# Tokens in runs of nine on two partition halves, early dummy matmuls, bf16 transposes of the token weight and a first token mix by source

## The chip, the cores and the metric

The kernel runs on one core of a Trainium2 chip. The metric is the device time of one execution in microseconds (us). TensorE (PE) multiplies, VectorE (DVE), ScalarE (ACT) and GpSimd (POOL) do elementwise work, and SyncE (SP) issues nearly all DMA. Every engine works through its own instructions in a fixed order that a small scheduler inside the kernel file fixes before the run: an instruction that waits holds up everything behind it on its engine.

Each run is timed beside the kernel before on the same chip. A ratio is the mean time of a kernel's fast runs over the mean of the fast runs of before of the same rounds, so it is not quite the ratio of the medians that are quoted. Where one of a kernel's executions was in the slow state, the median quoted here is that of its fast ones; the recorded expectations still quote medians of all (410.1 and 406.3 us for runs 4 and 5).

## The reference

```python
# q, k, v: [8 batches, 8 heads, 576 tokens, 64], f32
kv  = einsum('bhsd,bhse->bhde', k, v)
out = einsum('bhsd,bhde->bhse', q, kv)
x   = out / sqrt(mean(out*out, -1) + 1e-6) * g_norm      # -> [8, 576, 512]
a1  = alpha1 * x + beta1
u   = x + lam * einsum('ts,bsd->btd', w_tok, a1)         # token mix, w_tok 576x576
a2  = alpha2 * u + beta2
y   = u + lam * (relu(a2 @ w_ch1) @ w_ch2)               # channel mix, 512 -> 2048 -> 512
```

## The kernel before

Operations are recorded with their inputs, outputs and an estimated cost, put in order by the scheduler, and only then emitted. 576 tokens do not fill partitions evenly: 512 of them go on 128 partitions in runs of four, and the other 64 are a tail on 64 partitions, with packets of 256 bytes.

```python
def load_main(tile, key, src, b, hs, at=None):          # 128 partitions, 1 KB packets
    P.op("SP", 0.6, lambda e: e.dma_start(
        tile[:, hs].rearrange("p h c d -> p h (c d)"),
        src[b, hs, 0:512, :].rearrange("h (p c) d -> p h (c d)", c=4)), ...)

def load_tail(tile, key, src, b, lo, at=None):          # 64 partitions, 256 B packets
    P.op("SP", 0.7, lambda e: e.dma_start(
        tile[lo:lo + 64, :, :], src[b, :, 512:576, :].rearrange("h s d -> s h d")), ...)
```

From batch 2 on, q is split in two bf16 parts (`qs`: high part on ACT, rest on DVE or POOL) and transposed by DMA (`qt <- qs`). The product of k and v (`kv`) is evicted as two bf16 parts too (`kvd`), by ACT and DVE. Behind q times kv come a norm, a multiplication that makes the input of the token mix (`rt`), and the token mix.

```python
def split_q(b):
    for c in range(5):
        ...
        P.op("ACT", act_us(512), lambda e, ...: copy(e, hi, src), r=kin, w=[kh])
        P.op(dve_pool(512), 0, lambda e, ...: e.tensor_tensor(      # DVE or POOL
            out=lo, in0=src, in1=hi, op=ALU.subtract), r=kin + [kh], w=[kl])
...
P.op(dve_pool(64 * m), 0, lambda e: e.tensor_tensor(                # rt: DVE or POOL
    out=r_, in0=x, in1=eb, op=ALU.mult), ..., pri=-100)
...
P.op("SP", 0.6, lambda e: e.dma_start(out[b, c:512:4, :], x), r=keys, dma_us=0.8)   # one store
```

The scheduler's choice between two engines, its model of a DMA and its dummy matmuls (which fill PE's idle time before the first channel mix, once a zeroed tile `wz` is there):

```python
mine = t + o.cost[e] + (self.spare if e == "DVE" and "POOL" in o.eng else 0.0)
...
if at + o.cost[e2] < mine: return True                   # the other engine is better
...
dma_free = max(dma_free, t) + pick.lat                   # loads
pick.end = dma_free + 2.0
```

Of the kernel before, what the change touches and what calls it, by code (L numbers as in the profile page):

```python
# [22 lines left out]
class Op:  # L23
    __slots__ = ("eng", "cost", "fn", "deps", "alloc", "tiles", "pri", "idx",
                 "start", "end", "pos", "waits", "inc", "lat", "ring", "clock")

    def __init__(self, eng, cost, fn, pri, idx):
        self.eng, self.cost, self.fn, self.pri, self.idx = eng, cost, fn, pri, idx
        self.deps = set()
        self.alloc, self.tiles = [], []  # L30
        self.start = self.end = self.pos = None
        self.waits, self.inc, self.lat, self.clock, self.ring = [], False, None, None, None
# [3 lines left out]


# [10 lines left out]
class Prog:  # L48
# [20 lines left out]
    def op(self, eng, cost, fn, r=(), w=(), pri=0.0, dma_us=None, at=None):  # L69
# [4 lines left out]
        if at is not None:  # L74
            o.pri = at
        self.ops.append(o)
        for key in r:
# [24 lines left out]
    def hasten(self, targets):  # L102
# [11 lines left out]
        for o, way in rank.items():  # L114
            if o not in targets and o.eng != "SP":
                o.pri = -1000.0 - way

    def schedule(self):
# [25 lines left out]
        def place(tile, t):  # L144
# [5 lines left out]
            c = [b for b in range(8) if bank_ok(b, t)]  # L150
            if not c:
                return None
# [9 lines left out]
        def better_elsewhere(o, e, t):  # L162

            mine = t + o.cost[e] + (self.spare if e == "DVE" and "POOL" in o.eng else 0.0)
            for e2 in o.eng:
# [8 lines left out]
                if at + o.cost[e2] < mine:  # L174
                    return True
            return False

        while left:
            progressed = False
            for e, q in queues.items():  # L180
                while q and free[e] <= t + 1e-9:
                    pick = None
                    first = self.warm and self.warm[0].start is None
                    cands = q[:self.pe_window] if e == "PE" and not first else q[:400]
                    for o in cands:
# [6 lines left out]
                    if pick is None and e == "PE" and first:  # L192

                        tile = self.ptile(1)
                        pick = self.op("PE", 0.22, lambda e, tile=tile: self.warm[1](e, tile),
# [23 lines left out]
                    if pick.lat is not None:  # L219
                        if e == "SP":  # L220
                            dma_free = max(dma_free, t) + pick.lat
                            pick.end = dma_free + 2.0
                        else:
                            pick.end = t + pick.lat + 2.3
# [106 lines left out]
def bass_transnormer_attn__then__resmlp_affine_kernel(  # L331
# [15 lines left out]
    with ExitStack() as stack:  # L347
# [5 lines left out]
        with nc.sbuf_tensor("qtr", [128, 20, 128], F32R) as qtr:  # L353
            pass
# [5 lines left out]
        wz = sb("wz", [128, 512], BF16)  # L360
        smask = sb("smask", [128, 128], BF16)
        emask = sb("emask", [33, 128], BF16)
        ab2 = sb("ab2", [128, 8], F32)
        b2hl = sb("b2hl", [128, 4, 2], BF16)
        bias = sb("bias", [128, 16], F32)
        e1_bc = sb("e1_bc", [128, DM], F32)
# [3 lines left out]
        eps = sb("eps", [128, 1], F32)  # L370
        kf = sb("kf", [128, NH, 4, DH], F32)
        vf = sb("vf", [128, NH, 4, DH], F32)
        qf = sb("qf", [128, NH, 4, DH], F32)
        kft = sb("kft", [128, NH, DH], F32)
        qft = sb("qft", [128, NH, DH], F32)
# [19 lines left out]
        erow = stg[0:33, 1, 0:2, :]  # L395
        ebf = stg[0:33, 1, 2, 0:256].bitcast(BF16)
        pcol = stg[0:8, 2, 3, 0:128]
        grow = stg[0:1, 2, 3, 128:192]
        ones = stg[0:1, 2, 3, 192:320]
        wst, wst2 = hst[:, 0:2048], hst[:, 2048:2880]  # L400
# [31 lines left out]
        def load_main(tile, key, src, b, hs, at=None):  # L432
            P.op("SP", 0.6, lambda e: e.dma_start(
                tile[:, hs].rearrange("p h c d -> p h (c d)"),
                src[b, hs, 0:512, :].rearrange("h (p c) d -> p h (c d)", c=4)),
                w=[(key, a) for a in halves(hs)],
                dma_us=2.8 * (hs.stop - hs.start) / 8, at=at)

        def load_tail(tile, key, src, b, lo, at=None):
            P.op("SP", 0.7, lambda e: e.dma_start(  # L440
                tile[lo:lo + 64, :, :], src[b, :, 512:576, :].rearrange("h s d -> s h d")),
                w=[key], dma_us=0.55, at=at)

        def load_kv(b, parts=ALL, at=None):
            for i, hs in enumerate(parts):
                for tile, src, n in ((kf, k, "k"), (vf, v, "v")):
                    load_main(tile, n + "f", src, b, hs, at=at and at(n, i))
                    if i == 0:
                        load_tail(kft, n + "ft", src, b, 0 if n == "k" else 64,
                                  at=at and at(n + "t", i))  # L450

        def load_q(b, parts=ALL, at=None):
            for i, hs in enumerate(parts):
                load_main(qf, "qf", q, b, hs, at=at and at("q", i))
                if i == 0:
                    load_tail(qft, "qft%d" % (b % 2), q, b, 64 * (b % 2),
                              at=at and at("qt", i))

        def round_kv(b, parts=ALL):
            for i, hs in enumerate(parts):  # L460
                m = 256 * (hs.stop - hs.start)
                aa = halves(hs)
                for src, dst, lo, n in ((kf, kr, 0, "k"), (vf, vr, 64, "v")):
                    o, s = dst[:, 0:4, hs, :], src[:, hs].rearrange("p h c d -> p c h d")
                    ot, st = dst[0:64, 4, hs, :], kft[lo:lo + 64, hs]
                    P.op(act_dve(m, 1.7) if b < R32 else "DVE", dve_us(m, 1.7),
                         lambda e, o=o, s=s: copy(e, o, s),
                         r=[(n + "f", a) for a in aa], w=[(n + "r", a, 0) for a in aa])
                    P.op(act_dve(m // 4, 1.7) if b < R32 else "DVE", dve_us(m // 4, 1.7),
                         lambda e, o=ot, s=st: copy(e, o, s),  # L470
                         r=[n + "ft"], w=[(n + "r", a, 1) for a in aa])

        def split_q(b):

            lo_, par = 64 * (b % 2), b % 2
            for c in range(5):
                rows = slice(0, 128) if c < 4 else slice(lo_, lo_ + 64)
                src = qf[:, :, c, :] if c < 4 else qft[rows]
                hi, lo = qs[rows, c, :, 0, :], qs[rows, c, :, 1, :]
                kin = [("qf", 0), ("qf", 1)] if c < 4 else ["qft%d" % par]  # L480
# [15 lines left out]
        def qt_groups(b):  # L496

            def group(a, cp):
                t = P.ptile(1)
                lo = 64 * (b % 2)  # L500

                def f(e):
                    for i in range(4 if cp < 2 else 2):
                        if cp < 2:
                            m = e.transpose(t.flat()[:, 128 * i:128 * i + 128],
                                            qf[:, 4 * a + i, 2 * cp:2 * cp + 2, :].rearrange(
                                                "p c d -> p (c d)"), ident[:])
                        else:
                            h = 4 * a + 2 * i
                            m = e.transpose(t.flat()[:, 64 * i:64 * i + 64],  # L510
                                            flat(qft[lo:lo + 64, h:h + 2, :]),
                                            ident[lo:lo + 64, lo:lo + 64])
                    return m
                P.op("PE", 0.131 * (4 if cp < 2 else 2), f,
                     r=["ident", ("qf", a) if cp < 2 else "qft%d" % (b % 2)], w=[t])
                if cp < 2:
                    o = qtr[:, 8 * cp + 4 * a:8 * cp + 4 * a + 4, :].rearrange("p h s -> p (h s)")
                    s = lambda: t.flat()
                else:
                    o = qtr[:, 16 + 2 * a:18 + 2 * a, lo:lo + 64]  # L520
                    s = lambda: t.flat()[:, 0:128].rearrange("p (h s) -> p h s", h=2)
                P.op(act_dve(512 if cp < 2 else 128), 0, lambda e: copy(e, o, s()),
# [725 lines left out]
```

## Time and profile before

403.41 us median of three runs (403.21 to 404.55). What matters of the profile:

| | before |
|---|---|
| first channel-mix matmul (L850) | 58.21 us |
| first q times kv product of batch 2 (L614, the first 64-wide one on `kvd`) | 110.17 us |
| from there to the end of the span (400.7 us) | 290.5 us |
| landing of q's transposes, median | 3.8 us |

The page of before: busy time of PE, then the span in 40 slices of 10 us: PE's busy tenths, the granted PE clock in tenths, and what DMA moved; last the chain of waits that ended last, by engine.

```profile
PE 371.5 (93%) x2430; PEld 217.2 (54%) x2222; DVE 243.9 (61%) x355; ACT 154.4 (39%) x267; POOL 140.1 (35%) x105
PE   0999999899499999989999999989999999999995
PEclk9999999999889999999999999999999999999999
GB/s 205 318 315 332 281 353 350 17 131 138 200 290 200 150 101 114 207 149 190 147 210 123 107 101 196 199 39 106 81 78 26 106 52 2 26 119 27 2 52 79
...
PE 75%; DVE 11%; DMA 7%; issue 3%; ACT 1%; SPq 1%
```

PE is busy 93% of the time, and the DMA is near its full rate in the first 70 us (it reaches 353 GB/s). The chain is three quarters PE. Whether PE's time is well spent is told only by the length of its instructions. The timeline of PE before (start in us, length in us, line, operation, operands, count, and in brackets the idle time before it with what ended it):

```profile
9.64 2.50 PE L536 MATMUL ps<-vr,kr 128*128 128x256 f32 x10 [3.42 <-ACT vr L422]
...
44.85 2.64 PE L536 MATMUL ps<-vr,kr 128*128 128x256 f32 x20
...
58.21 1.04 PE L850 MATMUL ps<-a2t,w 128*128 128x256 bf16 x8
```

Ten kv products of 128x256 take 2.50 us at 9.64 us, and twenty take 2.64 us at 44.85 us: the first stage runs at half clock. The clock row shows 9 there all the same: the record of the clock begins at 42 us in this trace.

The timeline of DVE before, where it waits ahead of batch 2's products:

```profile
97.24 0.69 DVE L891 TENSOR_TENSOR xm<-ps,xm 128x512 f32<-128x512 f32 x1 [0.40 <-PE ps L882]
104.25 1.83 DVE L484 TENSOR_TENSOR qs<-qf,qs 128x512 bf16<-128x512 f32 x2 [6.32 <-ACT qs L422]
106.00 0.60 DVE L568 TENSOR_TENSOR kvd<-ps,kvd 64x128 bf16<-64x128 f32 x2
```

DVE is free at 97.9 us, and batch 2's two kv products are done on PE at 98.4 and 100.5 us. But a piece of batch 3's q split stands in front of their eviction (`kvd`) and waits 6.32 us.

### The profile page before, as it was taken

The page shows a single profiled execution, that of the slowest core. Times are in us where ns is not written, and L with a number is a line of the kernel's source. Part 1 is how long each engine was busy: PE and PEld are TensorE (multiplying, and loading weights), DVE is VectorE, ACT ScalarE, POOL GpSimd, SP SyncE. Part 2 cuts the span into 40 slices and gives each one's busy share as a digit, 9 for nine tenths or more (in the row PEclk, how much of TensorE's full clock was granted, in tenths as well). Part 3 has the DMA queues.
Part 4 walks back from the last instruction along what each step waited for, and adds up shares of the span by engine and source line. Part 5 has one row for each costly group of instructions (what it writes and reads, how often), then busy time and mean ns, then how long its engine had stood idle before and what let it go on. Part 6 is the DMA issues. An engine that isn't in the chain of part 4 may idle for free.

```text
span 400.7 us, 5755 instructions
## 1 busy us (share of the span) xinstructions
PE 371.5 (93%) x2430; PEld 217.2 (54%) x2222; DVE 243.9 (61%) x355; ACT 154.4 (39%) x267; POOL 140.1 (35%) x105
## 2 busy tenths in 40 slices
PE   0999999899499999989999999989999999999995
PEld 0775576446277346534765455435774465446642
DVE  6545879995579715994677628982783448350021
ACT  1345646800557004830465006801670048105600
POOL 3434538791317600492036400870062203420000
PEclk9999999999889999999999999999999999999999
DMA  8999999058799533967495337913340410050012
GB/s 205 318 315 332 281 353 350 17 131 138 200 290 200 150 101 114 207 149 190 147 210 123 107 101 196 199 39 106 81 78 26 106 52 2 26 119 27 2 52 79
DMA packets 94713, 59.25 MB, mean 148 GB/s; under 512 B 60817, under 2 KB 85401, under 8 KB 94688
## 3 DMA queue, kind: packets, MB, share of 16 engines
q1 hardware_dynamic: 94656, 58.88, 57.0%
q8 instruction: 18, 0.29, 0.3%
q14 instruction: 7, 0.06, 0.0%
q10 hardware_dynamic: 32, 0.02, 0.0%
HBM read 38.05 MB, written 9.44 MB: 119 GB/s over the span
## 4 chain that ended last, share of the span: by engine, by line
PE 75%; DVE 11%; DMA 7%; issue 3%; ACT 1%; SPq 1%
PE ps L882 27%; PE ps L835 13%; PE ps L820 10%; PE ps L713 7%; PE ps L536 5%; DMA qt<-qs 3%; DVE w L1154 2%; PE ps L614 2%; DVE qs L484 2%; PE ps L324 2%; DMA qf<-in_q_dram 2%; PE ps L1049 2%; DMA kft<-in_v_dram 2%; PE ps L926 2%; DVE rt L683 1%
## 5 line engine op out<-in xcount | busy, mean ns | idle before, releaser
L882 PE MATMUL ps<-w,ht 128*128 128x512 bf16 x559 | 126.8, 379 | 1.0
L809 ACT ACTIVATE ht<-ps,bias 128x640 bf16<-128x640 f32 (+2 forms) x114 | 82.1, 729 | 46.9 <-PE ps L835 35.3
L882 PEld LDWEIGHTS ps<-w,ht 128*128 128x128 bf16 x576 | 55.2, 98 | 63.8
L835 PE MATMUL ps<-a2t,w 128*128 128x320 bf16 x512 | 73.9, 304 | 6.3 <-DVE kvd L568 4.2
L891 DVE TENSOR_TENSOR xm<-ps,xm 128x512 f32<-128x512 f32 x32 | 22.1, 691 | 71.8 <-PE ps L882 71.6
L835 PEld LDWEIGHTS ps<-a2t,w 128*128 128x128 bf16 x512 | 49.8, 99 | 27.6 <-DVE kvd L568 4.6
L685 POOL TENSOR_TENSOR xm<-xm,g_bc 128x1024 f32<-128x1024 f32 (+1 forms) x18 | 40.2, 2236 | 51.6 <-DVE rt L683 50.8
L484 POOL TENSOR_TENSOR qs<-qf,qs 128x512 bf16<-128x512 f32 x15 | 22.5, 1501 | 93.3 <-ACT qs L422 92.9
L820 PE MATMUL ps<-a2t,w 128*128 128x512 bf16 x231 | 53.0, 379 | 0.5
L563 ACT ACTIVATE kvd<-ps 64x128 bf16<-64x128 f32 x24 | 6.5, 271 | 105.3 <-PE ps L536 105.1
L713 PE MATMUL ps<-rt,wt 128*128 128x512 bf16 x172 | 39.3, 379 | 4.7 <-DVE xm L695 2.5
L820 PEld LDWEIGHTS ps<-a2t,w 128*128 128x128 bf16 x240 | 22.8, 98 | 25.8
L713 PEld LDWEIGHTS ps<-rt,wt 128*128 128x128 bf16 x175 | 16.7, 98 | 26.4 <-DVE xm L695 4.0
L695 DVE TENSOR_TENSOR xm<-ps,xm 128x512 f32<-128x512 f32 x32 | 21.2, 686 | 15.5 <-PE ps L713 11.8
L657 DVE TENSOR_REDUCE small<-sq 128x16 f32<-128x1024 f32 (+3 forms) x27 | 25.2, 935 | 8.3 <-ACT sq L655 8.2
L536 PE MATMUL ps<-vr,kr 128*128 128x256 f32 x160 | 26.1, 315 | 3.4 <-ACT vr L422 3.4
L699 POOL TENSOR_TENSOR a2b<-xm,a_bc 128x512 bf16<-128x512 f32 x14 | 18.7, 1337 | 20.7 <-DVE xm L695 20.4
L536 PEld LDWEIGHTS ps<-vr,kr 128*128 128x128 f32 x160 | 22.9, 207 | 5.2 <-ACT vr L422 3.5
L655 ACT ACTIVATE sq<-ps 128x1024 f32<-128x1024 f32 (+3 forms) x27 | 21.6, 799 | 10.0 <-PE ps L324 6.7
L683 DVE TENSOR_TENSOR rt<-xm,e_bc 128x1024 bf16<-128x1024 f32 (+1 forms) x16 | 23.9, 1494 | 0.2
L679 DVE TENSOR_TENSOR xm<-ps,small 128x1024 f32<-128x1024 f32 (+1 forms) x18 | 19.7, 1102 | 0.3
L810 DVE TENSOR_SCALAR ht<-ps,bias 128x640 bf16<-128x640 f32 (+2 forms) x18 | 13.7, 761 | 10.0 <-PE ps L820 5.3
(113 smaller groups left out, 376.7 us busy)
## 6 DMA issues: line engine op xcount, KB each, us to landing
stg<-in_moe_w_ch_dram SPq DMA_DIRECT2D x8, 1024.0 KB, 12.0
out_dram<-xm SPq DMA_DIRECT2D x32, 256.0 KB, 2.4
kf<-in_k_dram SPq DMA_DIRECT2D x7, 1024.0 KB, 6.2
vf<-in_v_dram SPq DMA_DIRECT2D x7, 1024.0 KB
qf<-in_q_dram SPq DMA_DIRECT2D x7, 1024.0 KB, 7.0
kf<-in_k_dram SPq DMA_DIRECT2D x2, 512.0 KB, 6.1
kft<-in_k_dram SPq DMA_DIRECT2D x8, 128.0 KB, 6.5
vf<-in_v_dram SPq DMA_DIRECT2D x2, 512.0 KB, 7.4
```

The lines of the kernel that those rows point to most:

```text
L484: P.op(dve_pool(512), 0, lambda e, hi=hi, lo=lo, src=src: e.tensor_tensor(out=lo, in0=src, in1=hi, op=ALU.subtract), r=kin + [kh], w=[kl])
L536: m = e.matmul(o, flat(kr[:, c, 2 * pr:2 * pr + 2, :]), flat(vr[:, c, 4 * a:4 * a + 4, :]), start=(c == 0), stop=(c == 4))
L655: P.op("ACT", act_us(64 * m), lambda e: e.activation(sqv, raw(), ACT.Square), r=[t], w=[("sq", sqs)])
L657: P.op("DVE", dve_us(64 * m), lambda e: e.tensor_reduce(out=smv, in_=sqv, axis=AX.X, op=ALU.add), r=[("sq", sqs)], w=[("sm", sms)], pri=-20)
L683: lambda e: e.tensor_tensor(out=r_, in0=x, in1=eb, op=ALU.mult),
L685: P.op("POOL", pool_us(64 * m), lambda e: e.tensor_tensor(out=x3, in0=x3, in1=gb, op=ALU.mult), r=xk + ["g"], w=xk, pri=-50)
L713: m = e.matmul(t.flat(), wt[:, ws, tok_col(b, c):tok_col(b, c) + 128], rt[:, ws, :], start=(sc == 0), stop=(sc == 4))
L809: return e.activation(dst, src(), ACT.Relu, bias=bi)
L820: m = e.matmul(t.flat(), w1[:, dj, 128 * fj:128 * fj + 128], a2t[:, dj, 0:512], start=(dj == 0), stop=(dj == 3))
L835: m = e.matmul(t.ap()[:, i, 0:320], w1[:, dj, 128 * fj:128 * fj + 128], a2t[:, dj, 320 * i:320 * i + 320], start=(dj == 0), stop=(dj == 3))
L882: m = e.matmul(t.flat(), ht[:, fj, 128 * c:128 * c + 128], w2[:, fj, :], start=(fj == 0), stop=(fj == 15))
L891: P.op("DVE", dve_us(512), lambda e: e.tensor_tensor(out=x, in0=t.flat(), in1=x, op=ALU.add), r=[t] + keys, w=keys)
```

## The change

Its intent: no more tails of 256-byte packets, by giving each run of nine consecutive tokens to two partitions 64 apart, five tokens on one and four on the other; a released PE clock from the start, by dummies that need only the identity matrix; shorter transposes of `w_tok` (cast to bf16 first); and the first channel mix earlier, by running the first token mix source by source as sources become ready, and by putting batch 1's kv products and q transposes behind that channel mix. The core of the diff, cut (the cuts are marked):

```diff
-        def load_main(tile, key, src, b, hs, at=None): ...
-        def load_tail(tile, key, src, b, lo, at=None): ...
+        def load(n, b, parts=ALL, at=None):
+            ...
+                for x in range(2):                      # two loads, 64 partitions each
+                    sl = own(b, x)                      # 5 or 4 of a run's 9 tokens
+                    P.op("SP", 0.6, lambda e, ...: e.dma_start(
+                        tile[64 * x:64 * x + 64, hs, sl, :].rearrange("p h c d -> p h (c d)"),
+                        src[b, hs].rearrange("h (i n) d -> i h (n d)", n=9)[
+                            :, :, 64 * lo:64 * (lo + ns)]), ...)
...
-                    P.op("SP", 0.6, lambda e: e.dma_start(out[b, c:512:4, :], x), r=keys, dma_us=0.8)
+                    for y in range(2):
+                        P.op("SP", 0.6, lambda e, y=y: e.dma_start(
+                            out[b, 5 * y + c:576:9, :], x[64 * y:64 * y + 64, :]), r=keys, dma_us=0.4)
...
-            mine = t + o.cost[e] + (self.spare if e == "DVE" and "POOL" in o.eng else 0.0)
+            def cost(e):
+                return o.cost[e] + (self.spare if e == "DVE" and "POOL" in o.eng else 0.0)
+            mine = t + cost(e)
...
-                if at + o.cost[e2] < mine:
+                if at + cost(e2) < mine:
...
+                    if e == "SP" and q[0].pri < -900.0:
+                        cands = q[:1]                   # early loads in strict order
...
-                            dma_free = max(dma_free, t) + pick.lat
-                            pick.end = dma_free + 2.0
+                            dma_free = max(dma_free, t + 1.25) + pick.lat
+                            pick.end = dma_free + 1.3
...
-        run([tok_by_source(0), ut_first()])
-        load_kv(1, ...); load_q(1, ...)
-        round_kv(1)
+        run([tok_by_source(0), ut_first(), tok_groups(0)])
+        load_kv(1, ...); load_q(1, ...)
+        u0 = P.lastw[("a2t", 0)] + P.lastw[("a2t", 2)]
+        round_kv(1, HALVES, u0)                         # batch 1 behind the first channel mix
...
-            return e.matmul(t.flat(), wz[:, 0:128], wz[:], start=True, stop=True)
+            i2 = ident[:].bitcast(BF16)
+            return e.matmul(t.flat()[:, 0:256], i2[:, 0:128], i2, start=True, stop=True)
```

(Cut: the casts of `w_tok` and its bf16 transposes, the slots of the run-of-nine layout, the parameter rows, PSUM banks of the dummies, priorities.)

## The prediction

> **What bounds the kernel now.** The page gives PE 93% busy, but its first stage is slow. The timeline shows the first channel-mix matmul (L850) only at 58.2 us of 400.7. From 9.6 to 42 us PE is busy without a gap, at half speed: ten 128x256 kv matmuls (L536) take 2.50 us there, and twenty take 2.50 us at 45 us. (The Trainium skill, "TensorE: Matmul & The Clock Gate", Part 1: the array starts at half clock and sustained activity releases it; PEclk shows 1.0 here, so only durations tell it.) About 32 us of half-speed work is the bound until 42 us. The DMA is nearly full until 70 us (205, 318, 315, 332 GB/s in the first tens of us). DVE and POOL are full from 58 to 92 us. At 103 to 110 us PE waits: the split of batch 3's q stands before batch 2's kvd on ACT and DVE, and its load is issued only at 96.5 us and lands at 103.1. From there PE is nearly full.
>
> **What the change does.**
> - Dummies from the first us release the clock before the first kv product: 32 us of slow PE work shrink to about 16. PE stops being the first stage's bound.
> - w_tok is transposed in bf16 (five f32 transposes took 1.2 to 1.4 us), for ten POOL casts (128x512 took 0.61 us; 4 to 5 us together, partly hidden). Batch 1's kv products and q transposes (4.7 us) move behind the first channel mix.
> - Then the end is q's last half (4.9 MB loaded) and its chain: transposes, products, DVE's norm and scaling (about 7.5 us of 0.4 to 0.7 us pieces), last source of the token mix, residual, transposes: 15 to 17 us. The channel mix starts at 36 to 42 us, 16 to 22 us earlier.
> - Batch 2's q split now stands complete before batch 1's second scaling on POOL, so batch 3's q load and batch 2's kvd come earlier; the wait at 103 us should shrink.
>
> **What is given back.** All q, k, v and w_tok loads become pairs on 64 partitions. The tails go (dips to about 180 GB/s at 4, 7, 10, 19, 23 us), but the skill ("SBUF — State Buffer", Door 1) says that 64 partitions reach half of the ports: 196 GB/s at 1 MiB against 328, two halves hardly faster together. The dip at 19 us, where w_tok's 64-partition rest lands, hints at it. 15.5 MB on 64 partitions and 8.4 MB of w come before batch 3's q is in: at 340 GB/s no bound; at 225 PE waits for batch 1's q at 50 to 58 us, and batch 2's products start 7 us earlier instead of 20. The rest, from 110 us on, stays within 2 us.
>
> **Predicted:** 389 us, 8 in 10 between 379 and 401. Faster by over 2%: 0.78; within 2%: 0.18; slower: 0.04.
>
> **What shows each step.** Kv products of 125 ns from the first on; first 128x256 channel-mix matmul at 36 to 42 us; GB/s of the first 20 us (over 300: loads unharmed; near 220: ports); a PE gap before batch 1's q transposes; first 64-wide qk·v matmul of batch 2 at 88 to 103 us (before 110.2); work after that as long as before (290 us).
>
> **What would make it wrong.** Loads below 220 GB/s; waits on SP, which issues in strict order; casts and PSUM evictions on ACT behind q's last half longer than 17 us; the clock falling back in new gaps; a new DVE order blocking kvd worse than before.

## The result and the profile after

432.86 us median of four fast runs (431.07 to 436.2) against 403.31 for before in the same rounds: ratio 1.0745, 95% interval 1.0665 to 1.0824. The change makes the kernel 7% slower; 389 us had been predicted.

The page of after, the same rows (slices of 10.9 us):

```profile
PE 385.6 (89%) x2496; PEld 223.5 (51%) x2288; DVE 239.7 (55%) x358; ACT 151.5 (35%) x264; POOL 145.7 (34%) x114
PE   5999655969969869997999699979999999999995
PEclk9679957787988989998999699999999999999999
GB/s 182 221 332 209 197 195 238 194 203 147 205 92 224 192 158 107 77 203 166 173 98 217 131 108 90 119 192 79 109 92 56 73 72 26 2 84 75 0 50 73
...
PE 56%; DMA 24%; DVE 5%; SPq 5%; POOL 5%; ACT 2%; issue 2%; POOLq 0%; DVEq 0%
```

DMA moves about 200 GB/s for a hundred microseconds, where before it moved up to 353, and PE has idle slices and slices at a lowered clock until 250 us. DMA's share of the chain rises from 7 to 24%. The timeline of PE after:

```profile
2.02 4.02 PE L1225 MATMUL ps<-ident 128*128 128x256 bf16 x18 [2.02 <-POOL ident L1011]
...
6.91 1.05 PE L1225 MATMUL ps<-ident 128*128 128x256 bf16 x8
10.51 2.50 PE L548 MATMUL ps<-vr,kr 128*128 128x256 f32 x10 [2.55 <-DVE vr L436]
...
21.11 2.50 PE L548 MATMUL ps<-vr,kr 128*128 128x256 f32 x10
...
46.81 3.66 PE L870 MATMUL ps<-a2t,w 128*128 128x256 bf16 x32
54.17 1.12 PE L839 MATMUL ps<-a2t,w 128*128 128x512 bf16 x3 [3.71 <-ACT ht L828]
60.39 1.89 PE L839 MATMUL ps<-a2t,w 128*128 128x512 bf16 x4 [5.09 <-ACT ht L828]
```

The dummies start at 2 us and get faster (0.22 us each, then 0.13), but then PE waits 2.55 us for data, and both halves of the kv products take 2.50 us as before: the clock is not held. The first channel mix comes at 46.8 us, 11 us earlier, but stands still at once: it waits for its own relus on ACT. The timeline of ACT after shows why:

```profile
52.05 1.48 ACT L435 ACTIVATE kr<-kf 64x256 fp32r<-64x256 f32 x2 [5.21 <-DMA kf<-in_k_dram]
53.44 0.46 ACT L828 ACTIVATE ht<-ps,bias 128x256 bf16<-128x256 f32 x1
59.11 0.72 ACT L435 ACTIVATE vr<-vf 64x256 fp32r<-64x256 f32 x2 [5.22 <-DMA vf<-in_v_dram]
59.86 1.57 ACT L828 ACTIVATE ht<-ps,bias 128x256 bf16<-128x256 f32 x4
```

Casts of batch 1's k and v stand in front of the relus (`ht`) and wait 5.2 us each for their loads. The same happens once more just ahead of batch 2's first product. ACT and then DVE, in this order:

```profile
121.17 1.15 ACT L435 ACTIVATE qs<-qf 128x512 bf16<-128x512 f32 x2 [4.34 <-DMA qf<-in_q_dram]
122.35 1.23 DVE L502 TENSOR_TENSOR qs<-qf,qs 128x512 bf16<-128x512 f32 x1 [4.56 <-ACT qs L435]
```

Batch 3's q split still stands in front of batch 2's `kvd`, as in before, but its load now lands only at 121 us (before 103): DVE gets to `kvd` at 123.5 us (before 106.0), though the kv products are done on PE by 120.3.

The median from issue to landing (last column, us) of after's w loads and of its q transposes; before the same two were 12.0 and 3.8 us:

```profile
stg<-in_moe_w_ch_dram SPq DMA_DIRECT2D x8, 1024.0 KB, 18.9
qt<-qs SPq DMA_TRANSPOSE x30, 7.6
```

The first q times kv product of batch 2 starts at 129.3 us (before 110.2), and from there to the end of the span (434.2 us) it takes 304.9 us (before 290.5). So 19 us are lost in the front and 14 behind it, in the profiled executions (after's was its slowest, so the sum is some 4 us more than the medians differ by). A balance of PE's time in the two traces says the same in another way. "Useful" is PE's busy time less that of the dummies, "idle" is the span less PE's busy time:

| us | useful | dummies | idle | span |
|---|---|---|---|---|
| before | 367.2 | 4.3 | 29.2 | 400.7 |
| after | 372.6 | 13.0 | 48.6 | 434.2 |

### The profile page after: what moved, and what is told of

Its sections match the earlier page's. It is cut to its first block, busy times and chain, and to the rows that moved or that the text cites. A ratio compares the mean times of both kernels' runs of the same rounds, so it can differ in the third digit from the quotient of the medians.

```text
span 434.2 us, 5947 instructions
## 1 busy us (share of the span) xinstructions
PE 385.6 (89%) x2496; PEld 223.5 (51%) x2288; DVE 239.7 (55%) x358; ACT 151.5 (35%) x264; POOL 145.7 (34%) x114
## 4 chain that ended last, share of the span: by engine, by line
PE 56%; DMA 24%; DVE 5%; SPq 5%; POOL 5%; ACT 2%; issue 2%; POOLq 0%; DVEq 0%
PE ps L903 24%; PE ps L854 11%; DMA qt<-qs 9%; PE ps L839 7%; PE ps L727 7%; DMA qf<-in_q_dram 6%; DMA stg<-in_moe_w_ch_dram 5%; DMA ht<-in_moe_w_tok_dram 3%; SPq L459 3%; PE ps L548 3%; POOL ht L436 2%; PE ps L626 2%; PE ps L339 1%; ACT qs L435 1%; DVE qs L502 1%
## 5 line engine op out<-in xcount | busy, mean ns | idle before, releaser
L903 PE MATMUL ps<-w,ht 128*128 128x512 bf16 x556 | 130.3, 387 | 8.0 <-ACT ht L828 3.9
L828 ACT ACTIVATE ht<-ps,bias 128x640 bf16<-128x640 f32 (+2 forms) x107 | 76.8, 729 | 53.9 <-PE ps L854 38.4
L854 PE MATMUL ps<-a2t,w 128*128 128x320 bf16 x512 | 76.4, 309 | 8.0 <-ACT ht L828 8.0
L839 PE MATMUL ps<-a2t,w 128*128 128x512 bf16 x230 | 58.7, 406 | 15.4 <-ACT ht L828 14.6
L854 PEld LDWEIGHTS ps<-a2t,w 128*128 128x128 bf16 x512 | 50.5, 101 | 30.5 <-ACT ht L828 9.3
L697 POOL TENSOR_TENSOR rt<-xm,e_bc 128x1024 bf16<-128x1024 f32 x6 | 14.1, 2356 | 124.1 <-DVE xm L693 124.1
L839 PEld LDWEIGHTS ps<-a2t,w 128*128 128x128 bf16 x240 | 23.4, 103 | 44.5 <-ACT ht L828 16.9
L699 POOL TENSOR_TENSOR xm<-xm,g_bc 128x1024 f32<-128x1024 f32 (+1 forms) x18 | 39.9, 2217 | 13.2 <-DVE rt L697 12.2
L727 PE MATMUL ps<-rt,wt 128*128 128x512 bf16 x180 | 42.0, 389 | 1.1 <-POOL rt L697 0.9
L435 ACT ACTIVATE qs<-qf 128x512 bf16<-128x512 f32 (+1 forms) x30 | 18.2, 625 | 34.0 <-DMA qt<-qs 23.9
L709 DVE TENSOR_TENSOR xm<-ps,xm 128x512 f32<-128x512 f32 x32 | 21.5, 686 | 15.3 <-PE ps L727 14.6
L829 DVE TENSOR_SCALAR ht<-ps,bias 128x512 bf16<-128x512 f32 (+2 forms) x25 | 19.0, 769 | 9.9 <-PE ps L854 5.2
L502 DVE TENSOR_TENSOR qs<-qf,qs 128x512 bf16<-128x512 f32 (+1 forms) x17 | 16.5, 981 | 14.2 <-ACT qs L435 13.9
## 6 DMA issues: line engine op xcount, KB each, us to landing
stg<-in_moe_w_ch_dram SPq DMA_DIRECT2D x8, 1024.0 KB, 18.9
```

What stands on the lines that cost most here:

```text
L435: return e.activation(out, in_, ACT.Identity)
L699: P.op("POOL", pool_us(64 * m), lambda e: e.tensor_tensor(out=x3, in0=x3, in1=gb, op=ALU.mult), r=xk + ["g"], w=xk, pri=-50)
L709: P.op("DVE", dve_us(512), lambda e: e.tensor_tensor(out=x, in0=t.flat(rows), in1=x, op=ALU.add), r=[t] + xk, w=xk, pri=-100)
L727: m = e.matmul(t.flat(), wt[:, ws, tok_col(b, c):tok_col(b, c) + 128], rt[:, ws, :], start=(sc == 0), stop=(sc == 4))
L828: return e.activation(dst, src(), ACT.Relu, bias=bi)
L839: m = e.matmul(t.flat(), w1[:, dj, 128 * fj:128 * fj + 128], a2t[:, dj, 0:512], start=(dj == 0), stop=(dj == 3))
```

## The experiments

Eighteen kernels ran. The first four ask about the loads, the next eight about order and clock, the last six about what the order does. "Whole loads" stands for loads on 128 partitions.

### 1. Loads by themselves

A kernel of nothing but loads and stores, in phases of 8.4 MB each (9.4 in the runs of nine, 4.2 of w beside 8.4 in the mixed one, 4.2 in a phase of stores): whole loads of 1 KB packets; pairs of loads on partitions 0 to 63 and 64 to 127; pairs on the even and the odd partitions; loads on partitions 0 to 63 alone; the runs of nine; halves mixed with whole loads of w; then stores. Its output is wrong, which doesn't matter for the time.

```python
def rows(b, x, step):                       # half of the 128 partitions
    return slice(64 * x, 64 * x + 64) if step == 1 else slice(x, 128, 2)
...
phases = (all128(sp), halves(sp, k, 1), halves(sp, v, 2), lower(sp), runs9(sp),
          mixed(sp), store(sp, None), store(sp, 1), tails(sp))
```

> No compute, wrong result on purpose: phases of loads alone, each ended before the next begins. Theory ports (a load whose rows lie on one half of the partitions, 0-63 or 64-127, gets half the rate, and alternating halves do not fill each other's gaps): eight 128-partition loads of 8.4 MB in about 24 us (345 GB/s, 1024 B packets of 46 to 51 ns); the same bytes as alternating blocks of 64 partitions in about 40 us (near 205 GB/s, packets near 80 ns); as alternating even and odd partitions in about 24 us again; all into the lower half in about 41 us; runs of nine as in the changed kernel, 9.4 MB, about 45 us; w loads among halves slowed too (2048 B packets well over 88 ns). Rival count (half-size transfers, or twice as many issues, are what is slow): even and odd partitions as slow as blocks. Rival run length (1280 B runs with a 2304 B pitch are what is slow): blocks of 64 with 1024 B packets as fast as 128 partitions, only the runs of nine slow.

Windows inside these phases, in this order but for the tails (from:to, length, engine columns, the clock, the DMA share, and last the GB/s):

```profile
5.00:25.00 20.00, 0.00 (x0) 1.00 1.10 349
30.00:65.00 35.00, 0.00 (x0) 1.00 1.12 224
70.00:94.00 24.00, 0.00 (x0) 1.00 1.06 341
98.00:134.00 36.00, 0.00 (x0) 1.00 1.13 215
142.00:180.00 38.00, 0.00 (x0) 1.00 1.12 220
186.00:236.00 50.00, 0.00 (x0) 1.00 1.11 236
241.00:251.00 10.00, 0.00 (x0) 1.00 1.01 375
255.00:274.00 19.00, 0.00 (x0) 1.00 0.89 204
```

Whole loads move 349 GB/s, pairs of contiguous halves 224, pairs of even and odd partitions 341, one half alone 215. So it is neither the number of loads nor 64 partitions as such, nor the length of the packets (runs of nine: 220), but which partitions they are: two halves in flight together move hardly more than one (224 against 215). The Trainium skill, "SBUF — State Buffer", section "Door 1: The DMA port swizzle", gives 16 ports, with partitions 0 to 63 on eight of them, and a rule by which bits of the partition number pick the port; even partitions reach all 16 by that rule. The rates of this run agree with that. Stores behave alike: 375 GB/s whole, 204 as blocks of 64 rows (which are also half as large; run 5 tells the two apart). In the trace a packet of 1 KB took 51 ns on average in whole loads and 82 ns in halves. w's 2 KB packets took 113 ns on average between half loads (the middle one 93, one in twenty over 185). This run has none of w by itself, but run 4 below and after, with the same order of work, compare them: 100 ns on average in the first 90 us with whole loads, 112 with half loads. So w's loads pay a little too, though they stay whole.

### 2 and 3. Before with half loads, and with even and odd halves

The kernel before, each whole load of q, k and v issued as two loads, all orders of instructions unchanged.

```diff
-            P.op("SP", 0.6, lambda e: e.dma_start(
-                tile[:, hs]..., src[b, hs, 0:512, :]...),
+            P.op("SP", 0.6, lambda e: [e.dma_start(
+                tile[r, hs]..., src[b, hs, 0:512, :]...[r])
+                for r in (slice(0, 64), slice(64, 128))],          # run 2
+                # run 3: (slice(0, 128, 2), slice(1, 128, 2))
```

> The kernel before, every engine's order unchanged, with each 128-partition load of q, k, v issued as two loads of partitions 0-63 and 64-127. Theory ports: slower, 415 to 430 us, GB/s near 200 in the first tens of us, 1024 B packets near 80 ns. Rival count: slower as well. Rivals run length and order (the changed kernel is slow because of its new order of work, not its loads): within 1% of before.

> As the run before, but the two loads take the even and the odd partitions. Theory ports: within 1.5% of before (402 to 409 us), packets near 50 ns. Rival count: as slow as with halves.

Contiguous halves: 431.52 us (430.02 to 434.57), ratio 1.0682 (1.061 to 1.0754). Even and odd halves: 404.52 us, ratio 1.0003 (0.9958 to 1.0048). Half loads alone cost before as much as the whole change costs it, and the same number of loads on alternate partitions costs nothing.

### 4. After with whole loads

The kernel after, each pair of half loads replaced by one whole load and one tail in before's layout of tokens, `w_tok` too. The order of instructions is the same on every engine (POOL's casts of `w_tok` are cut differently). Stores stay pairs of 64 rows.

```diff
-                        tile[64 * x:64 * x + 64, hs, sl, :]..., src[b, hs]... n=9 ...
+                        if x == y: ... tile[64 * y:64 * y + 64, hs, slot(b, 4), :] ... # tail
+                        else:      ... tile[:, hs, y:4 + y, :] ... src[b, hs, 0:512, :] ... c=4
```

> The changed kernel with the same instruction order on all engines, but its pairs of 64-partition loads replaced by one 128-partition load and a 64-partition tail each, in the token layout of the kernel before (w_tok as well; stores stay pairs of 64 rows). Theory ports: most of the loss comes back and the rest of the change shows: 383 to 398 us, first channel mix at 36 to 42 us, over 300 GB/s in the first 30 us. Rival order: stays over 420 us.

408.95 us, median of three fast runs (407.69 to 411.25; a fourth was slow), ratio 1.0124 (1.0063 to 1.0185): 24 us less than after, and still slower than before, between the two expectations. The first channel mix now starts at 43.73 us, 14.5 earlier than before; batch 2's first product starts at 106.9 us (before 110.2), only 3 earlier; and from there to the end it takes 302.3 us, 12 more. From the first channel mix to batch 2's first product after takes 82.5 us and this run 63.2; PE stands idle there for 21.8 and 8.0 us, and the clock record shows half clock for 30.3 and 10.2 us. So half loads are the larger cause, but not the only one, and a gain of 14.5 us in the front goes somewhere.

### 5, 6 and 7. Stores, and the scheduler's DMA constants

Run 5 is run 4 with each pair of stores on even and odd partitions. Run 6 is before with only the two new DMA constants. Run 7 is run 5 with the old ones.

```diff
# run 5
-    out[b, 256 * y + c:256 * y + 256:4, :], x[64 * y:64 * y + 64, :]
+    out[b, 4 * y + c:512:8, :], x[y:128:2, :]
# run 6, on before (run 7 does the reverse on run 5)
-    dma_free = max(dma_free, t) + pick.lat;         pick.end = dma_free + 2.0
+    dma_free = max(dma_free, t + 1.25) + pick.lat;  pick.end = dma_free + 1.3
```

> The kernel after with 128-partition loads (410.1 us), its order of instructions unchanged on every engine; only each pair of output stores is now the even and the odd partitions instead of partitions 0 to 63 and 64 to 127[...]. Theory S (half-rate stores delay the transposes of q behind them, and this is what the steady state of that kernel loses against before): 397 to 402 us, time from the first q product of batch 2 to the end back near 290 us, landing of the q transposes back from 6.3 to about 4 us. Rival M (the new static order, from the changed DMA model and priorities, makes ACT, DVE and POOL wait for DMA): 407 to 412 us, landing of the q transposes still about 6 us.

> The kernel before with nothing changed but the two constants that the static scheduler assumes for DMA (loads issue 1.25 us later and land 1.3 instead of 2.0 us after; ACT-issued 3.0 instead of 2.3), so only the order of instructions differs. Theory M (the new model gives a worse order): slower than before, 408 to 415 us. Rival: order from the constants costs little, 400 to 406 us.

> As the run with even and odd stores, with the scheduler's two DMA constants set back to those of before. Theory M: 393 to 402 us, steady state near 290 us. Rival (constants of no consequence, the loss is in the stores or in the other changes): same as the run with even and odd stores within 3 us.

Run 5: 404.98 us, median of three fast runs, ratio 1.0051 (0.9981 to 1.0122). A 2 KB packet of a store, 149 ns in the middle in run 4 from 130 us on, takes 82 here. By medians the stores are worth about 4 us of 409 (the intervals of the two ratios overlap), but the tail from batch 2's first product is still 298.6 us and q's transposes still land in 6.2 us: theory S explains a part, not the loss. Run 6: 399.03 us, ratio 0.9888 (0.9818 to 0.9958). Run 7: 414.24 us (three fast runs), ratio 1.0266 (1.0199 to 1.0332). Theory M in the form "the new constants make a worse order" falls twice: they help before by 1.1%, and taking them away from the changed kernel costs it 9.3 us by the medians. (To set back the new rule for the choice between DVE and POOL alone could not be tried, so there is no run of it: with the old one the scheduler gets stuck and finds no order for the changed kernel. What that rule costs by itself stays open.)

### 8 to 12. The clock

Run 8 is run 5 with 30 more dummies directly in front of the first kv product. Run 9 is before with dummies alone: 20 and 28 ahead of the first kv product, and 3 in front of each of 27 groups of matmuls up to the token weight's sums; no other instruction moves. Run 10 has 1 in place of 3, run 11 adds 3 per group to run 8, run 12 puts run 9's dummies in run 6. A dummy goes into the PSUM bank that the group writes next, so it needs no wait of its own.

```diff
+        for o in pe[2:stop]:                    # PE's operations in their order
+            if o.alloc and ... :                # those that write a fresh bank
+                def f(e, fn=o.fn, tile=o.alloc[0]):
+                    for _ in range(3):
+                        e.matmul(tile.flat()[:, 0:256], wy[:, 0:128], wy[:], start=True, stop=True)
+                    return fn(e)
```

> As the run with even and odd stores, with 30 more dummy matmuls right in front of the first kv product. If sustained bf16 matmuls release the clock and the f32 products after them hold it, the first ten kv matmuls take 1.25 us instead of 2.50 and so do the second ten. If f32 work does not hold the clock, the first ten start at 125 ns each and later f32 work falls back to 250 ns within some us. If the f32 products are slow at any clock this early, they take 2.50 us although the dummies take 0.11 to 0.13 us each. The whole kernel: within 5 us of the run without them.

> The kernel before, the order of all real work unchanged on every engine, plus dummies alone: 20 bf16 matmuls of 128x256 in front of the first transpose, 28 in front of the first kv product, and 3 in front of each of about 25 groups of matmuls in the f32 stage up to 42 us (one more memset on DVE feeds them). Theory C (what was missing for the 16 us that I had expected of the clock is only that f32 work does not hold it; with bf16 matmuls between, it stays released): kv products of 125 ns in both halves, the f32 stage is over 8 to 14 us earlier, and the kernel runs 392 to 399 us. Rival D (the first stage was never bound by PE; the loads set it): products fast, PE idle appears in their place, 400 to 405 us. Rival (the clock is not held even so): kv of 250 ns in the second half, 403 to 410 us because of the added work.

> As the run before with 3 dummies per group, but 1 per group. If a share of about an eighth of bf16 work is enough to hold the clock, kv products of the second half take 125 ns; if not, the clock falls back after the first half, as it did with no dummies between (from 15 us on).

> The kernel after with 128-partition loads, even and odd stores and 30 dummies in front of the first kv product, plus 3 dummies in front of each group of the f32 stage. Theory C: the clock stays released from 5 us on, the second kv half takes 1.25 us, the first channel mix comes 2 to 5 us earlier (40 to 42 us), the whole 396 to 401 us. Rival D (loads set the first channel mix): it stays at 44 us, and the whole is 401 to 405 us.

> The kernel before with the new DMA constants of the scheduler (399.0 us) and the dummies of the first run of this call. Theory C: 387 to 395 us. Rival D: 397 to 401 us.

Run 8: 403.14 us, a single run. The timeline of its PE:

```profile
10.58 1.43 PE L556 MATMUL ps<-vr,kr 128*128 128x256 f32 x10
11.85 1.42 PE L533 MATMUL ps<-ident,qf 128*128 128x128 f32 x12
13.20 2.20 PE L954 MATMUL ps<-w 1*128 1x512 f32 x6
...
20.04 2.50 PE L556 MATMUL ps<-vr,kr 128*128 128x256 f32 x10
```

The first ten kv products now take 1.43 us, so f32 products are fast when the clock is released; but ten us later, with no bf16 work in between, the second ten take 2.50 us again. The clock record of the trace has half clock from 15.3 to 25.6 us. All its steps, in every run, lie whole multiples of 3.41 us apart. That is the window that the Trainium skill, "TensorE: Matmul & The Clock Gate", Part 1, gives for the gate. A stall of 2 to 4 us can be followed by such a window at half clock: in run 5 half clock follows at 128.9 us on the idle time of 2.41 us that is shown below, and at 173.3 us on one of 3.75 us, but not on one of 2.88 us that ends at 263.5 us.

Run 9: 405.1 us, ratio 1.0037 (0.9967 to 1.0106). Its PE:

```profile
10.35 1.45 PE L537 MATMUL ps<-vr,kr 128*128 128x256 f32 x10 [1.30 <-ACT vr L423]
...
18.89 1.44 PE L537 MATMUL ps<-vr,kr 128*128 128x256 f32 x10
```

Here both halves are fast (1.45 and 1.44 us). Ahead of the first channel mix PE's time for other work than dummies falls by 9 to 16 us (from 44.1 to 34.6 us by these instructions' own records, from 43.6 to 27.2 as PE's busy time less that of the dummies; the recorded ends of neighbours overlap, and the truth lies between). Over the whole kernel the difference is only 10.5 us (367.2 to 356.7). But the dummies between the groups have records of 13.5 us (81 of them; the 48 in front take 6.9 us that PE would have idled), the first channel mix comes only 3.5 us earlier, at 54.7 us, and batch 2's first product starts at 110.6 us, as before. With 1 per group (run 10, 403.46 us, a single run) the second half is at 2.48 us again. Run 11: 416.31 us, ratio 1.0313 (1.0236 to 1.0389). The same 3 per group did not hold the clock there (half clock from 21.1 to 31.3 us), and with its 75 more dummies the first channel mix came at 55.2 us instead of 44.2: a miss of both theories. The stretch from batch 2's first product to the end is 10.6 us longer than in run 8 with the same order of work; the clock record shows half clock for 22.7 us of it, against 3.5 in run 8. Run 12: 400.27 us, ratio 0.9888 (0.9791 to 0.9985), the same as run 6 without them. In these runs a released clock in the first stage is worth nothing in the end, once its dummies are paid.

What these runs show together is in the fourth and fifth columns here, from the traces:

| run | median us | ratio to before | first channel mix | batch 2's first product | from there to the end |
|---|---|---|---|---|---|
| before | 403.3 | 1 | 58.2 | 110.2 | 290.5 |
| after | 432.9 | 1.0745 | 46.8 | 129.3 | 304.9 |
| 4: after, whole loads | 409.0 | 1.0124 | 43.7 | 106.9 | 302.3 |
| 5: and even and odd stores | 405.0 | 1.0051 | 45.0 | 107.0 | 298.6 |
| 6: before, new DMA constants | 399.0 | 0.9888 | 55.6 | 106.9 | 289.1 |
| 8: 5 with 30 dummies | 403.1 | single run | 44.2 | 106.5 | 294.7 |
| 9: before with dummies | 405.1 | 1.0037 | 54.7 | 110.6 | 291.0 |
| 11: 8 with dummies between | 416.3 | 1.0313 | 55.2 | 110.5 | 305.3 |

With whole loads the first channel mix starts anywhere from 43.7 to 58.2 us, and batch 2's first product at 106.5 to 110.6. An earlier first channel mix alone brings the end no nearer in any of them. Part of it is only a move: in the changed order PE has work behind the first channel mix that it had in front of it before (batch 1's kv products and q transposes).

### 13 to 16. What stands in front of what

Two candidates were left. K: pieces of the next batch's q split stand in front of `kvd`, and wait for DMA. R: in the changed order POOL makes `rt`, the token mix's input, in nine places, some of them behind pieces of the q split (before: three, each a 64-partition piece, beside two of batch 0). The timelines of ACT, DVE, POOL and PE in run 5, in this order, show one such case:

```profile
126.27 0.63 ACT L435 ACTIVATE qs<-qf 128x512 bf16<-128x512 f32 x1 [3.51 <-DMA qt<-qs]
...
123.14 0.18 DVE L685 RECIPROCAL small<-small 64x8 f32<-64x8 f32 x1
126.93 0.69 DVE L509 TENSOR_TENSOR qs<-qf,qs 128x512 bf16<-128x512 f32 x1 [3.61 <-ACT qs L435]
127.54 0.68 DVE L701 TENSOR_TENSOR xtl<-ps,small 64x512 f32<-64x512 f32 x1
...
128.01 1.15 POOL L509 TENSOR_TENSOR qs<-qf,qs 128x512 bf16<-128x512 f32 x1 [3.74 <-ACT qs L435]
129.24 1.75 POOL L705 TENSOR_TENSOR rt<-xtl,e_bc 64x512 bf16<-64x512 f32 x1
...
129.06 1.89 PE L911 MATMUL ps<-w,ht 128*128 128x512 bf16 x4 [2.41 <-DVE ht L837]
131.05 5.32 PE L735 MATMUL ps<-rt,wt 128*128 128x512 bf16 x21
```

The reciprocal of the last norm is done at 123.3 us. What is left to the token mix are two short multiplications. But ACT waits 3.51 us for a transpose to free `qs`, DVE's next instruction is the second half of that piece, POOL's next the same for another piece, and the token mix (L735) starts at 131.05 us, after an idle time of 2.41 us on PE.

```diff
# K: a batch's q split waits for kvd of the batch before it
+                for o in (o1, o2):              # the two operations of split_q
+                    o.deps.update(y for a in range(2) for h in range(2) for i in range(3)
+                                  for y in P.lastw.get(("kvd", a, h, i), ()))
# R: rt stays on DVE
-                P.op(dve_pool(64 * m) if b else "DVE", dve_us(64 * m),
+                P.op("DVE", dve_us(64 * m),
```

Runs 13, 14 and 15 are run 5 with K, with R, with both. Run 16 is run 6 (before with the new constants) with K. Nothing is taken away: K adds a wait, R binds an engine, and the scheduler makes a new order.

> The changed kernel with whole loads and even and odd stores (406.3 us), with one more dependency: the split of a batch's q waits for the kvd evictions of the batch before, so kvd stands first on ACT and DVE. Theory K (the wait of kvd behind batch 3's q split is what sets the start of batch 2's products): first 64-wide qk times v product of batch 2 at 99 to 103 us instead of 107, the whole 399 to 404 us. Rival (something else sets it): start within 2 us of 107, the whole 403 to 410 us.

> The changed kernel with whole loads and even and odd stores, with the multiplication that feeds the token mix kept on DVE in every batch (before has it there but for three 64-partition pieces; the changed order has nine on POOL). Theory R (these stand on POOL behind pieces of the q split that wait for transposes, and PE then waits): from the first 64-wide product of batch 2 to the end 288 to 293 us instead of 298.6, the whole 396 to 402 us. Rival (it is the DMA landing of the transposes itself that PE waits for, whichever engine multiplies): 296 to 304 us for that stretch, the whole 403 to 410 us.

> Both of the two edits above. If both theories hold, the gains add: start of batch 2's products at 99 to 103 us and 288 to 293 us from there, the whole 390 to 396 us. If K alone, 399 to 404; if R alone, 396 to 402; if neither, 403 to 410 us.

> The kernel before with the new DMA constants of the scheduler (399.0 us), with kvd in front of the next batch's q split as in the first run of this call. Theory K: batch 2's products start at 100 to 104 us instead of 106.9, the whole 392 to 396 us. Rival: 397 to 402 us.

| run | median us | ratio to before (95%) | first channel mix | batch 2's first product | from there to the end |
|---|---|---|---|---|---|
| 5 | 405.0 | 1.0051 (0.9981 to 1.0122) | 45.0 | 107.0 | 298.6 |
| 13: K | 395.2 | 0.9822 (0.9786 to 0.9859) | 43.1 | 105.8 | 289.0 |
| 14: R | 402.1 | 0.9996 (0.9956 to 1.0036) | 43.8 | 107.1 | 292.5 |
| 15: both | 392.3 | 0.9758 (0.97 to 0.9816) | 43.4 | 105.0 | 285.4 |
| 16: before, new constants, K | 389.8 | 0.9673 (0.9628 to 0.9717) | 55.9 | 104.5 | 284.2 |

K is worth about 10 us and R 3, and together they give 13 (9, 2 and 12 by the ratios). R alone is not clear of noise: its interval overlaps that of run 5. K's gain is clear, and so is that of both. But K's mechanism is not quite the one that had been expected: batch 2's first product comes only 1.2 us earlier, not 4 to 8, and in run 5 `kvd` is held up by the next batch's q split in batch 2 alone.

The gain lies behind it. In run 5 each q split of a later batch is placed so early that ACT waits for the transposes of the batch before to free `qs` (3.5, 4.4, 2.9 and 3.5 us, the longest), in front of norms and relus that PE needs; with K the split comes one batch later, and no such wait is over 1 us. From batch 2's first product on, PE's idle times (over 0.15 us) add up to 12.5 us in run 5, 6.4 in run 13, 3.1 in run 15 and 1.4 in run 16 (before 5.4, after 14.8), and the clock record shows half clock for 7.1, 1.5, 0.1 and 0 us (before 3.8, after 18.2). The place shown above for run 5, now in run 15, DVE and then PE:

```profile
119.71 0.18 DVE L688 RECIPROCAL small<-small 64x8 f32<-64x8 f32 x1
119.93 0.68 DVE L704 TENSOR_TENSOR xtl<-ps,small 64x512 f32<-64x512 f32 x1
120.64 0.73 DVE L708 TENSOR_TENSOR rt<-xtl,e_bc 64x512 bf16<-64x512 f32 x1
...
122.06 5.34 PE L738 MATMUL ps<-rt,wt 128*128 128x512 bf16 x24
```

From the start of the reciprocal to the end of `rt` it is 1.7 us instead of 7.9, and the token mix starts without a wait (of these runs only one execution each is profiled). The median landing of q's transposes falls with it, from 6.2 us in run 5 to 4.5 in run 15 (4.6 with K alone, 4.2 with R alone), so these runs do not tell the time of the transposes from the order that asks for them.

Run 16, faster than had been expected, is at least as fast as run 15 (389.8 against 392.3 us; the intervals of the ratios just meet), though its first channel mix starts 12.5 us later and it has none of the change's layout, early dummies, bf16 transposes or mix by source. The front of the change gains nothing that these runs can show.

### 17 and 18. Dummies in idle time, and half loads in the mended order

Run 17 is run 16 with the 48 early dummies alone, which fit in PE's idle time. Run 18 is the kernel after, half loads and half stores and all, with K and R; its order on PE, ACT and DVE is that of run 15.

> The fastest kernel so far (before with the new DMA constants and kvd first, 389.8 us), the order of all real work unchanged, with 20 dummies in front of the first transpose and 28 behind it, in time that PE now spends idle, and none between the f32 groups. If the clock is what the first stage lacks and idle dummies are free: the first kv products and transposes at full clock, 4 to 6 us of PE time saved up to about 16 us, the whole 384 to 387 us. If the first stage is set by loads and evictions: the same within 1 us, 388 to 391 us.

> The changed kernel itself, with its loads and stores on 64 partitions, with the two edits of order (kvd first, multiplication on DVE): the same order as the run with both edits (392.3 us), which has whole loads and even and odd stores. If half loads cost what they did before the order was mended (432.9 against 406.3 us): 412 to 420 us. If the order was what made them costly: 394 to 402 us.

Run 17: 389.53 us in six runs, ratio 0.9651 (0.9613 to 0.969), within 0.3 us of run 16. The kv products are fast in both halves, and the first channel mix comes at 55.48 us instead of 55.92:

```profile
10.43 1.47 PE L540 MATMUL ps<-vr,kr 128*128 128x256 f32 x10
...
16.34 1.41 PE L540 MATMUL ps<-vr,kr 128*128 128x256 f32 x10
```

PE's idle time falls from 21.5 to 15.4 us, and its dummies rise from 3.6 to 11.4: they fill time, and that is all.

Run 18: 405.79 us, median of three fast runs (403.61 to 406.68), ratio 1.0042 (0.9981 to 1.0103); its profiled run was a slow one and is not used. Against run 15 half loads and stores cost 13.5 us (11 by the ratios), in the old order they had cost 28 (432.9 against 405.0). The run lies between the two expectations (402 and 412 us): both are true in part. As a table of medians:

| | half loads and stores | whole loads, even and odd stores |
|---|---|---|
| order of the change | 432.9 (after) | 405.0 (run 5) |
| with K and R | 405.8 (run 18) | 392.3 (run 15) |

Late loads and an order in which engines wait for loads and transposes make each other worse: either cure alone gives 27 to 28 us, both together 41.

## Why the prediction was wrong

The predicted 389 us is close to what the change takes with whole loads and a mended order (392.3 us). That is no credit to it: these are the two things that the prediction weighed and let pass.

- **The term that failed: "batch 2's products start 7 us earlier instead of 20"** for loads at 225 GB/s. The rate was read rightly (the loads ran at about 220 GB/s, run 1), and the skill's section had been quoted with its 196 against 328. But the term was mis-sized: batch 2's products start 19 us later, so the step is off by 26 us. The sum counted bytes against the moment at which PE needs them. It left out that w's whole loads land later between half loads (18.9 us after issue; 13.2 in run 4, with the same order), and that ACT, DVE and POOL work in order, so that a cast that waits for k or v holds the relus of a channel mix that has all its data (5.2 us twice in after), and batch 3's q split, waiting for its load until 121 us, holds batch 2's `kvd`. With nothing but whole loads in their place (run 4) batch 2's first product comes 22.4 us earlier. Run 2 shows how much half loads cost without any of the rest: 6.8%.
- **"The rest, from 110 us on, stays within 2 us" failed as well.** It measured 304.9 us after, and 298.6 with loads and stores mended, against 290.5. The order of ACT, DVE and POOL in later batches is not kept by a scheduler that has new costs and a new rule for choosing between DVE and POOL. The prediction had looked at the order for batch 3's q split and concluded "the wait at 103 us should shrink"; in after the wait is still there, 4.6 us long, and ends 18 us later than before; in run 5 DVE reaches that piece only at 100 us, and in later batches the q split waits for transposes ahead of norms and relus. Runs 13 to 15 show what this order costs, about 13 us.
- **"Dummies from the first us release the clock before the first kv product; 32 us shrink to about 16" failed.** Kv products took 250 ns in both halves. 26 dummies release the clock, but on an idle time of 2.55 us a window at half clock follows (10.2 to 13.6 us), and after one full window there is half clock again until 27.2 us; in run 8 f32 work alone runs at half clock for ten us. The size was not what failed: where dummies do hold the clock (run 9), PE's other work ahead of the first channel mix gets 9 to 16 us shorter, but the dummies between take most of that back, and the mix comes 3.5 us earlier.
- **"PE is the bound until 42 us", and the channel mix "16 to 22 us earlier" as a gain, failed as reasons.** With whole loads the channel mix did come 13 to 15 us earlier, a little less than said (without more dummies). But batch 2's first product hardly moved in any of the runs, and the fastest kernel has a late channel mix. PE being busy and slow in a stage does not make that stage the bound of the end.
- **Right:** `w_tok`'s bf16 transposes are short (20 take 1.9 us; five f32 ones had taken 1.4 at half clock, and take 0.9 at full clock in run 9), PE did wait for batch 1's q in after (4.5 us), and the list of what could go wrong named the clock falling back in new gaps and an order in which `kvd` is blocked worse than before. Naming a risk is not costing it: the chance given to slower was 0.04.
- **Still open:** what sets the start of batch 2's first product at 104.5 to 107 us in the mended kernels. K moved it by 1 to 2 us only. From the first channel mix to it PE's idle times add up to 6.9 us of 61.6 in run 15 and 2.6 of 48.6 in run 16, so there PE's own work, in its order, fills nearly all of it; what the loads still add in front of that no run here separates. Nor does a run take apart the pieces of the new order (the choice between DVE and POOL, the strict order of the first loads, the priorities).

## What to carry to other kernels

Before you count a layout's packets, ask which partitions each transfer touches: two transfers on contiguous halves ran at 64% of the rate of whole ones here, and on even and odd partitions at 98%. When a front stage is shortened, find the next point where all chains meet and ask what sets that; a gain that ended before it was worth nothing here. And when a static order changes, look on each in-order engine for prefetch work (here the next batch's q split) that stands in front of work that the matrix engine waits for: one added dependency was worth about 2% in both kernels, more than the 1.1% of the new DMA constants, the one part of the change that a run showed to help.

## What the Trainium skill lacked or had wrong

- "SBUF — State Buffer", section "Door 1: The DMA port swizzle": its rule fits the rates here in each case tried, but the page lists contiguous ranges only. Alternate partitions, 64 of 128, run at 341 GB/s against 224 for contiguous halves and 349 for whole loads (run 1), and cost before nothing (ratio 1.0003). Its 196 GB/s at 1 MiB is for one transfer; a row of half loads ran at 215 to 224, near the asymptote that the page gives (about 218).
- The same section has no figure for stores: 375 GB/s whole, 204 as blocks of 64 rows (run 1).
- No page that I read has a figure for whole loads beside half loads: w's 2 KB packets took 113 ns on average there in run 1, and in the first 90 us 112 in after against 100 in run 4, whose order is the same.
- "DMA: Bandwidth & Descriptors", section "Rules for kernel authors": "Two transfers to disjoint partition halves: Don't bother" holds for contiguous halves (224 GB/s); as even and odd halves two transfers are about as good as one (341 against 349).
- "TensorE: Matmul & The Clock Gate", Part 1: the window of 3.41 us agrees with every step of the clock records here. But its picture of a busy PE that gets the full clock does not cover f32 work as it is here: PE was busy from 9.6 to 34 us in before, and its kv products stayed at 250 ns (in after, though, one window at full clock, 13.6 to 17.0 us, follows on the first kv products, so these runs give no rule for f32 work); with three bf16 dummies of 0.13 us before each group they took 145 ns (run 9), with one not (run 10), and in run 11 three did not hold it. Part 4 says that transposes do not count as busy; that fits, but no run here tells transposes from f32 products.
- The same Part 1 warns that recorded clock events can be unreliable, but not of this case: before the first record a clock row can show full clock. Before's row shows 9 for the first 40 us, in which matmuls ran at half speed, so its mean of 0.991 is too high.
